# First stage of a fused attention and two-layer expert kernel: other places for weight conversions and input loads

## The chip, the cores and the metric

The kernel runs on one core of a Trainium2 chip. The metric is the device time of one execution in microseconds (us). Three runs of the kernel before the change gave 792.18, 792.83 (the median) and 796.73 us. The profile and every row below come from one profiled execution of 793.86 us, whose traced span is 792.0 us.

## The reference

Three layers follow each other; the output of one is the input of the next.

```
scores = q @ k.T / 8        # 4 batches, 8 heads, 576 tokens, 64 per head
                            # heads 0-3 see the last 32 tokens, heads 4-7 every fourth of the last 128
x = softmax(scores) @ v     # -> 2304 tokens x 512
x = (x @ w_a * (x @ w_b)) @ w_out          # 512 -> 1536 -> 512
e = argmax(normalised x @ expert_emb.T)    # 8 experts
out = gate * (relu(x @ w1[e]) @ w2[e])     # 512 -> 1024 -> 512
```

w_a, w_b and w_out arrive as 64-bit floating-point numbers, everything else as 32-bit ones. The kernel converts the 64-bit weights to 32 bits on the chip.

## The kernel before

**Batches and steps.** The work goes batch by batch. For batch b, `f_step(b, f, ...)` runs for the 12 blocks f of 128 hidden columns (n = 12 b + f numbers them through), and then `x1_run` multiplies by w_out. One `f_step` has four groups of 12 matmuls on TensorE, `mm(0,0)`, `mm(1,0)`, `mm(0,1)`, `mm(1,1)`: column half c of the weights (a or b) by token half hf, each product as three passes (high by high, high by low, low by high; lines 702 to 704). Each group fills one PSUM bank. `a_copy` (ACT, L739) empties the bank of the a half, `g_evac` (DVE, L745) multiplies it with the b half and so empties that bank; a later `g_lows` splits the product into a high part (ACT, L748) and a low part (POOL, L749).

**Attention inside the steps.** While batch b is in these steps, the attention of batch b + 1 is worked off in pairs of 64-query tiles (`AttnPair`; five pairs, the last one a single tile). In batch 0 a pair opens in an odd-numbered n (1, 3, 5, 7, 9: "even" in the code, since f - lag is even there) and goes on in the next. Its parts: `scores` (PE, into the banks sc and rps), `least_of` (maxima, DVE L536, then a small POOL operation, L544), `exp(i)` (four ACT exponentials per tile, L550), `norm(i)` (two small DVE operations, L557 and L558, then a POOL product, L559, over the tile s), `trans(i)` (four PE transposes into the single bank tp, L567, and an ACT copy out of it, L569), `av` (PE, L578), `oevac` (ACT L593, DVE L595). `trans(0)` stands in the second step of a pair, `trans(1)` at the head of the step after it. The attention of batch 0 itself runs ahead of the first step (class `Attn`, tiles j = 0 to 8, `trans` of tile i - 3 and `av` of tile i - 4 in turn i), with a few filler matmuls (`keep_warm`).

**Conversion of the weights, in batch 0 only.** `conv_load(i)` brings block i as 64-bit words (1024 KB). `conv_steps(i)` makes 32-bit numbers of it in four steps that `conv(cg, k)` takes k at a time: ACT scales the upper words in place (L640), DVE shifts (L642), DVE combines (L644), DVE combines again (L646). `conv_store` writes the result back to DRAM for the later batches. In step n, block n + 2 is converted; `ab_split(n+1)` splits the block converted in the step before into a high part (ACT, L660) and a low part (DVE, L661) in one of the two buffers "ab". The split of block 1 is done in step 0 in four parts, its low parts on POOL.

**What sets the order.** The order is written out by hand: every engine works its own instructions off strictly in the order of the code, and so does SP, which issues all loads and stores of this stage; a wait at the head of a queue holds all that is behind it. Semaphores between engines follow from the buffers. The PSUM banks and the bank tp exist once each. `load_qk` and `load_v` go through the input tiles (batch, third g): 832 KB and 576 KB each, two buffers each, so that a third one waits until an earlier tile has been used. `early_conv` converts blocks 0 and 1 during the attention of batch 0.

In the step that opens a pair ACT gets before the change: copy of `trans(1)`, L640, L660, L739, L593, L748, `exp(0)`, L748, L739; DVE gets L642, L661, maxima, L595, L644, L745, `norm(0)`, L745, L646.

Of the kernel before, what the change touches and what calls it, by code (L numbers as in the profile page):

```python
# [8 lines left out]
F32 = mybir.dt.float32  # L9
# [72 lines left out]
def fused_kernel(ctx: ExitStack, tc: tile.TileContext, qk, v, wab, wout, w1, w2, emb, tau, cst, msk, out, dbg=None):  # L82
# [279 lines left out]
    ap = ab_ctx.enter_context(tc.tile_pool(name="ab", bufs=2, side="right"))  # L362
    ld = attn_ctx.enter_context(tc.tile_pool(name="ld", bufs=2, side="right"))
# [9 lines left out]
    qkt, vt = {}, {}  # L373

    ld_seq = [(b, g) for b in range(B) for g in range(3)]
    ld_pos = [0, 0]

    def load_qk():
        if ld_pos[0] < len(ld_seq):
            b, g = ld_seq[ld_pos[0]]  # L380
            ld_pos[0] += 1
            qkt[b, g] = ld.tile([128, 4, 416], F32, tag="qk", name="qkt")
            nc.sync.dma_start(out=qkt[b, g], in_=qk[b, g])

    def load_v():
        if ld_pos[1] < len(ld_seq):
            b, g = ld_seq[ld_pos[1]]
            ld_pos[1] += 1
            vt[b, g] = ld.tile([96, 3, 512], F32, tag="v", name="vt")
            nc.sync.dma_start(out=vt[b, g], in_=v[b, g])  # L390

    x0 = {}
# [214 lines left out]
    def conv_load(i):  # L607
        if i < len(conv_src):
            if i < NF and i % 3 == 2:
                c64[i] = mp.tile([128, 2048], I32, tag="wo", name="c64w", bufs=1)  # L610
            elif i in (NF + 2, NF + 3):
                c64[i] = ap.tile([128, 2048], I32, tag="ab", name="c64a")
            else:
                c64[i] = cv.tile([128, 2048], I32, tag="c64", name="c64")
            nc.sync.dma_start(out=c64[i], in_=conv_src[i].bitcast(I32))
# [3 lines left out]
    def raw_tile(name):  # L619
        return mp.tile([128, 1024], F32, tag="raw", name=name, bufs=3)  # L620

    def conv_store():
        while conv_kept:
            keep, dst = conv_kept.pop(0)
            nc.sync.dma_start(out=keep, in_=dst)
# [24 lines left out]
    def conv(gen, n=4):  # L650
        for _ in range(n):
            next(gen, None)

    def ab_load(n):
        if NF <= n < n_ab:
            ab_raw[n] = raw_tile("abr")
            nc.sync.dma_start(out=ab_raw[n], in_=wab32[n % NF])
# [9 lines left out]
    def ab_split_part(n, q):  # L667
        if q == 0:
            ab_hl[n] = ab_tile()
        w = slice(256 * q, 256 * q + 256)  # L670
        split(ab_raw[n][:, w], ab_hl[n][0][:, w], ab_hl[n][1][:, w], eng=nc.gpsimd)
        if q == 3:
            ab_raw.pop(n)

    def ab_split(n):
        if n < n_ab:
            hl = ab_tile()
            split(ab_raw.pop(n), *hl)
            ab_hl[n] = hl
# [9 lines left out]
    def wo_split(n):  # L689
        if n < N_WO:  # L690
            if not wo_box:
                wo_box.append(mp.tile([128, 2, 2, 512], F32R, tag="wo", name="wo", bufs=1))
            hl = (wo_box[0][:, n % 2, 0, :], wo_box[0][:, n % 2, 1, :])
            w = slice(512 * (n % 2), 512 * (n % 2) + 512)
            split(wo_raw[n // 2][:, w], *hl, eng=nc.vector)
            if n % 2:
                wo_raw.pop(n // 2)
            wo_hl[n] = hl
# [9 lines left out]
    def ab_mm(n, acc, c, hf, k):  # L708
        hl = ab_hl[n]
        xh, xl = x0[n // NF]  # L710
        if k == 0:
            acc[c, hf] = ps.tile([128, HALF], F32, tag=f"mm{2 * hf + c}", name=f"mm{2 * hf + c}")
        w = slice((2 * k + c) * 128, (2 * k + c) * 128 + 128)
        t = slice(hf * HALF, hf * HALF + HALF)
        mm3(acc[c, hf], (hl[0][:, w], hl[1][:, w]), (xh[:, k, t], xl[:, k, t]), k == 0, k == 3)
# [7 lines left out]
    def f_step(b, f, pairs, extra, extra2):  # L723
        n = b * NF + f
        acc = acc_pre if n == 0 else {}
        lag = 1 if b == 0 else 0
        p, odd = divmod(f - lag, 2)
        cur = pairs[p] if 0 <= p < len(pairs) else None
        prv = pairs[p - 1] if not odd and 0 <= p - 1 < len(pairs) else None

        def mm(c, hf):
            for k in range(2 if (c, hf) in acc else 0, 4):
                ab_mm(n, acc, c, hf, k)

        kept = {}

        def a_copy(hf):
            kept[hf] = ap.tile([128, HALF], F32, tag="a", name="a")
            nc.scalar.activation(out=kept[hf], in_=acc[0, hf], func=AF.Copy)  # L739

        def g_evac(hf):
            g = ap.tile([128, HALF], F32, tag="g", name="g")
            c = hf * HALF + CARRY * (1 - b % 2)
            t = slice(c, c + HALF)
            nc.vector.tensor_tensor(out=g, in0=kept[hf], in1=acc[1, hf], op=ALU.mult)  # L745

            def low():
                nc.scalar.activation(out=g_hl[0][:, f, t], in_=g, func=AF.Copy)  # L748
                nc.gpsimd.tensor_tensor(out=g_hl[1][:, f, t], in0=g, in1=g_hl[0][:, f, t].bitcast(F32), op=ALU.subtract)  # L749

            g_low.append(low)

        if f - lag in (3, 6, 9):
            load_qk()
        if f - lag in (5, 8, 11):
            load_v()
        if f < NF - 2:
            ab_load(n + 2)
        if b == 0 and n < 10:
            conv_load(n + 4)  # L760
        if n == NF - 1:
            conv_load(NF + 2)
        if b == 0:
            conv_store()
        cg = iter(())
        if b == 0:
            cg = conv_steps(n + 2)
        if cur is not None and odd:
            conv(cg, 1)
            cur.exp(1)  # L770
            conv(cg, 1)
            cur.norm(1)
            conv(cg, 1)
        if prv is not None:
            prv.trans(1)
        if not odd or cur is None:
            conv(cg, 2)
        if n == 0:
            for q in range(4):
                ab_split_part(1, q)  # L780
        elif f < NF - 1:
            ab_split(n + 1)
        elif b == 0:
            wo_split(0)
        mm(0, 0)
        a_copy(0)
        if not odd:
            if cur is not None:
                cur.open()
            if prv is not None:  # L790
                prv.av()
            if cur is not None:
                cur.scores()
                cur.least_of()
            if prv is not None:
                prv.oevac()
            conv(cg, 1)
        g_lows()
        mm(1, 0)
        if cur is not None and not odd:  # L800
            cur.exp(0)
        g_evac(0)
        if cur is not None and odd:
            cur.trans(0)
        g_lows()
        for x in extra:
            x()
        mm(0, 1)
        a_copy(1)
        for x in extra2:  # L810
            x()
        mm(1, 1)
        if cur is not None and not odd:
            cur.norm(0)
        g_evac(1)
        del ab_hl[n]
        conv(cg)
# [347 lines left out]
    with tc.manual_schedule():  # L1165
# [17 lines left out]

        early_conv = conv_all()
        for i in range(NJ + LAG + 1):
            if i in (3, 6, 9):
                load_qk()
            if i in (4, 6, 9):
                load_v()
            if i == CONV1:  # L1190
                conv_load(1)
                nc.sync.dma_start(out=c_sb, in_=cst)
            if i == 6:
                conv_load(2)
            if i < NJ:
                gr[i].scores(early=True)
            if 1 <= i < NJ + 1:
                gr[i - 1].exp()
            if LAG <= i < NJ + LAG:
                gr[i - LAG].trans()  # L1200
                gr[i - LAG].tevac()
            if LAG + 1 <= i:
                gr[i - LAG - 1].av()
            keep_warm(N_WARM if i < 4 else N_WARM_LATE if i < WARM_TO else 0, "mm1" if (i + 1 - LAG) % 2 else "tp")
            if 1 <= i < NJ + 1:
                gr[i - 1].norm()
            if i == NJ + LAG:
                conv(early_conv, CONV_STEPS[i])
            if LAG + 1 <= i:
                gr[i - LAG - 1].oevac()  # L1210
            if i < NJ + LAG:
                conv(early_conv, CONV_STEPS[i])
            for q in range(4):
                if SPLIT0[q] == i:
                    ab_split_part(0, q)
            if i in PRE:
                for k in range(2):
                    ab_mm(0, acc_pre, PRE.index(i), 0, k)
        for _ in early_conv:
            pass  # L1220
        load_v()

        router = None
        for b in range(B):
# [10 lines left out]
            for f in range(NF):  # L1235
                extra = []
                extra2 = []
                if b == 1 and f == 0:
                    ebox.append(rbox_pool[0].tile([128, E1, DM], F32, tag="big", name="en_a"))
                    ebox.append(ap.tile([128, E - E1, DM], F32, tag="en_b", name="en_b", bufs=1))  # L1240
                    for t, e0 in zip(ebox, (0, E1)):
                        n = t.shape[1]
# [261 lines left out]
```

## Time and profile before

| | |
|---|---|
| runs | 792.18, 792.83, 796.73 us |
| profiled execution | 793.86 us, span 792.0 us |
| busy over the span | PE 774.6, PEld 723.5, DVE 518.8, ACT 410.1, POOL 206.2 us |
| opening, 0 to 62 us | PE busy 55.38 us, DVE 42.78, ACT 39.81, POOL 25.58; DMA 91% |
| rest of the first stage, 62 to 124 us | PE busy 62.00 us, DVE 52.48, ACT 42.96, POOL 27.20; DMA 77% |
| chain that ended last | PE 84% of the span, DMA 9%, issue 4%, DVE 1%, ACT 1% |

PE is TensorE's matmul side, PEld its weight loads, DVE VectorE, ACT ScalarE, POOL GpSimd, SP the queue that issues loads. Matmuls are pipelined and their ends are modelled, so a PE that is busy is not a PE at its peak. In rows of the timeline, the first number is the start in us from the span's start, the second the duration in us; a square bracket at the end gives the idle time of the engine just before and what ended it.

### The profile page before, as it was taken

The numbers are of one execution on the slowest core, as the hardware profiler recorded it, in microseconds if no ns is written. First come the engines' busy times: TensorE is split into PE (matmuls) and PEld (weight loads), VectorE is DVE, ScalarE is ACT, GpSimd is POOL, SyncE is SP. The second block draws the span as 40 slices with busy tenths as digits, with TensorE's granted clock in tenths as the row PEclk, the third lists the DMA queues.
The fourth block names the chain that finished last, engine by engine and source line by source line (L and its number), as shares of the span: only waits on it lengthen the run. The fifth ranks groups of instructions, "written<-read, shape, count | busy, mean of one in ns | idle before, by whom it ended". The sixth has DMA issues, their size and how long they took to land.

```text
span 792.0 us, 15979 instructions
## 1 busy us (share of the span) xinstructions
PE 774.6 (98%) x6122; PEld 723.5 (91%) x6122; DVE 518.8 (66%) x1155; ACT 410.1 (52%) x993; POOL 206.2 (26%) x251
## 2 busy tenths in 40 slices
PE   8989999999999999999999999999999999999995
PEld 4789998899999889999889999999898999999993
DVE  5788888758986228887627874455564566566570
ACT  5757774366653136665234443455463655665651
POOL 3454443023442204443222225331000001111110
PEclk9999999999999999999999999999999999999998
DMA  9987877497732323222152222635574554755720
GB/s 285 317 254 235 283 259 272 185 329 231 258 124 85 133 83 113 93 81 81 63 174 97 81 81 99 247 134 176 204 249 157 181 177 139 251 157 165 237 79 26
DMA packets 40294, 136.18 MB, mean 172 GB/s; under 512 B 4083, under 2 KB 4339, under 8 KB 37776
## 3 DMA queue, kind: packets, MB, share of 16 engines
q1 hardware_dynamic: 37120, 125.54, 48.4%
q0 software_dynamic: 3088, 9.52, 3.2%
q8 instruction: 50, 0.82, 0.4%
q14 instruction: 36, 0.29, 0.1%
HBM read 109.67 MB, written 25.80 MB: 171 GB/s over the span
## 4 chain that ended last, share of the span: by engine, by line
PE 84%; DMA 9%; issue 4%; DVE 1%; ACT 1%; POOL 0%; POOLq 0%; DVEq 0%; ACTq 0%
PE mm L702 13%; PE mm L703 12%; PE mm L704 12%; DMA out_dram<-yo,ixi 5%; PE xr L702 5%; PE xr L703 5%; PE xr L704 4%; PE hp L704 3%; PE hp L703 3%; PE hp L702 3%; PE av L578 2%; DMA c<-in_wab_dram 2%; PE ytp L703 2%; PE xm L704 2%; PE ytp L704 2%
## 5 line engine op out<-in xcount | busy, mean ns | idle before, releaser
L702 PE MATMUL mm<-x0h,ab 128*128 128x288 f32 x768 | 230.8, 301 | 1.0 <-DVE g L745 1.0
L704 PE MATMUL mm<-x0h,ab 128*128 128x288 f32 x768 | 226.5, 295 | 0.3 <-DVE ab L661 0.3
L703 PE MATMUL mm<-x0l,ab 128*128 128x288 f32 x768 | 226.2, 295 | 0.0
L702 PEld LDWEIGHTS mm<-x0h,ab 128*128 128x128 f32 x768 | 144.1, 188 | 3.5 <-DVE g L745 1.2
L704 PEld LDWEIGHTS mm<-x0h,ab 128*128 128x128 f32 x768 | 144.1, 188 | 0.9 <-DVE ab L661 0.5
L703 PEld LDWEIGHTS mm<-x0l,ab 128*128 128x128 f32 x768 | 144.2, 188 | 0.2
L749 POOL TENSOR_TENSOR gl<-g,gh 128x288 fp32r<-128x288 f32 x96 | 90.6, 946 | 131.6 <-ACT gh L748 128.6
L661 DVE TENSOR_TENSOR wl<-raw,wh 128x1024 fp32r<-128x1024 f32 x60 | 73.0, 1222 | 53.4 <-ACT wh L660 53.2
L661 DVE TENSOR_TENSOR wo<-wor,wo 128x512 fp32r<-128x512 f32 x60 | 47.0, 785 | 63.6 <-ACT wo L660 58.8
L660 ACT ACTIVATE wo<-wor 128x512 fp32r<-128x512 f32 x60 | 37.8, 631 | 86.0 <-PE xr L704 57.4
L1120 POOL DMA_INDIRECT out_dram<-yo,ixi x23 | 26.4, 1146 | 205.6 <-ACT yo L1119 160.3
L661 DVE TENSOR_TENSOR ab<-abr,ab 128x1024 fp32r<-128x1024 f32 x46 | 58.9, 1281 | 29.7 <-ACT ab L660 29.7
L745 DVE TENSOR_TENSOR g<-a,mm 128x288 f32<-128x288 f32 x96 | 43.2, 450 | 41.4 <-PE mm L704 17.0
L702 PE MATMUL hp<-xTh,wh 128*128 128x352 f32 (+6 forms) x224 | 68.9, 308 | 0.0
L748 ACT ACTIVATE gh<-g 128x288 fp32r<-128x288 f32 x96 | 42.9, 447 | 47.9 <-DVE g L745 47.4
L703 PE MATMUL hp<-xTl,wh 128*128 128x352 f32 (+6 forms) x224 | 67.7, 302 | 0.0
L704 PE MATMUL hp<-xTh,wl 128*128 128x352 f32 (+6 forms) x224 | 67.6, 302 | 0.0
L660 ACT ACTIVATE wh<-raw 128x1024 fp32r<-128x1024 f32 x64 | 67.1, 1054 | 0.0
L660 ACT ACTIVATE ab<-abr 128x1024 fp32r<-128x1024 f32 (+1 forms) x54 | 51.4, 961 | 23.2 <-PE mm L704 16.1
L702 PE MATMUL xr<-wo,gh 128*128 128x512 f32 x156 | 61.0, 391 | 0.0
L703 PE MATMUL xr<-wo,gh 128*128 128x512 f32 x156 | 60.9, 390 | 0.0
L704 PE MATMUL xr<-wo,gl 128*128 128x512 f32 x156 | 60.8, 390 | 0.0
(239 smaller groups left out, 1654.5 us busy)
## 6 DMA issues: line engine op xcount, KB each, us to landing
raw<-in_w_dram SPq DMA_DIRECT2D x64, 512.0 KB, 4.1
abr<-wab SPq DMA_DIRECT2D x36, 512.0 KB, 3.2
wor<-wout SPq DMA_DIRECT2D x24, 512.0 KB, 3.6
qkt<-in_qk_dram SPq DMA_DIRECT2D x12, 832.0 KB, 11.0
c<-in_wab_dram SPq DMA_DIRECT2D x8, 1024.0 KB, 11.4
vt<-in_v_dram SPq DMA_DIRECT2D x12, 576.0 KB
xs<-rows SPq DMA_DIRECT2D x8, 781.5 KB
wab<-abr SPq DMA_DIRECT2D x12, 512.0 KB, 6.4
```

What stands on the lines that cost most here:

```text
L578: nc.tensor.matmul(out=self.o[64 * p:64 * p + 64, pr, 64 * i:64 * i + 64], lhsT=t[:, jj, 64 * h:64 * h + 64], rhs=self.aT[i][:, pr, 64 * ( ...
L660: nc.scalar.activation(out=hi, in_=raw, func=AF.Copy)
L661: (eng or nc.vector).tensor_tensor(out=lo, in0=raw, in1=hi.bitcast(F32), op=ALU.subtract)
L702: nc.tensor.matmul(out=out_, lhsT=lh, rhs=rh, start=first, stop=False)
L703: nc.tensor.matmul(out=out_, lhsT=lh, rhs=rl, start=False, stop=False)
L704: nc.tensor.matmul(out=out_, lhsT=ll, rhs=rh, start=False, stop=last)
L745: nc.vector.tensor_tensor(out=g, in0=kept[hf], in1=acc[1, hf], op=ALU.mult)
L748: nc.scalar.activation(out=g_hl[0][:, f, t], in_=g, func=AF.Copy)
L749: nc.gpsimd.tensor_tensor(out=g_hl[1][:, f, t], in0=g, in1=g_hl[0][:, f, t].bitcast(F32), op=ALU.subtract)
L1120: nc.gpsimd.indirect_dma_start(out=out, out_offset=bass.IndirectOffsetOnAxis(ap=self.ixi[e][:m, t:t + 1], axis=0), in_=yo[:m, :], in_offse ...
```

## The change

It has three parts. The third v tile of batch 0 is put into a buffer of the kind "ab", so that it needs no free v buffer, and is loaded right behind the second. The loads of the second batch (its first v, and its second q/k tile) move behind the conversions of batch 0's attention, and its second v into step n = 2. In the steps of batch 0 the four conversion steps move: where a pair opens, L640 and L642 from ahead of `ab_split` to behind `exp(0)` and the first `g_evac`, and L644 from behind `oevac` to ahead of `norm(0)`; where a pair goes on, L640 from ahead of `exp(1)`, L642 from ahead of `norm(1)` and L644 from behind it, to behind `a_copy(0)` (L640 and L642) and the first `g_evac` (L644). L646 stays at the end of a step.

```diff
@@ load_v
-            vt[b, g] = ld.tile([96, 3, 512], F32, tag="v", name="vt")
+            if ld_pos[1] == 3:
+                vt[b, g] = ap.tile([128, 2048], F32, tag="ab", name="vt")[:96, :1536].rearrange("p (j c) -> p j c", j=3)
+            else:
+                vt[b, g] = ld.tile([96, 3, 512], F32, tag="v", name="vt")
@@ f_step
         if f < NF - 2:
             ab_load(n + 2)
+        if n == 2:
+            load_v()
...
         if cur is not None and odd:
-            conv(cg, 1)
             cur.exp(1)
-            conv(cg, 1)
             cur.norm(1)
-            conv(cg, 1)
         if prv is not None:
             prv.trans(1)
-        if not odd or cur is None:
+        if cur is None:
             conv(cg, 2)
...
             if prv is not None:
                 prv.oevac()
-            conv(cg, 1)
+            if cur is None:
+                conv(cg, 1)
+        elif cur is not None:
+            conv(cg, 2)
         g_lows()
         mm(1, 0)
         if cur is not None and not odd:
             cur.exp(0)
         g_evac(0)
+        if cur is not None:
+            conv(cg, 1 if odd else 2)
         if cur is not None and odd:
             cur.trans(0)
         g_lows()
...
         mm(1, 1)
         if cur is not None and not odd:
+            conv(cg, 1)
             cur.norm(0)
         g_evac(1)
         del ab_hl[n]
         conv(cg)
@@ attention of batch 0
-            if i in (3, 6, 9):
+            if i == 3:
                 load_qk()
-            if i in (4, 6, 9):
+            if i == 4:
+                load_v()
                 load_v()
             if i == CONV1:
                 conv_load(1)
+            if i == 6:
+                load_qk()
+                conv_load(2)
                 nc.sync.dma_start(out=c_sb, in_=cst)
-            if i == 6:
-                conv_load(2)
...
         for _ in early_conv:
             pass
+        load_qk()
         load_v()
```

## Rows read from the trace of the kernel before

**Rows 1.** Windows: stretch, length, busy us per engine, granted clock, DMA share, GB/s.
```profile
20.00:40.00 20.00, 18.48 (x219) 14.32 (x217) 14.55 (x39) 14.75 (x58) 9.29 (x15) 1.00 1.03 315
...
50.00:55.00 5.00, 3.44 (x25) 3.20 (x26) 4.78 (x9) 4.75 (x16) 3.91 (x4) 1.00 0.46 119
60.00:80.00 20.00, 20.00 (x249) 19.38 (x244) 17.44 (x32) 14.69 (x45) 9.04 (x11) 1.00 0.77 244
```

**Rows 2.** Timeline of PE: start, duration, line; idle before in brackets.
```profile
28.70 0.28 PE L474 MATMUL av<-aT,vt 96*64 96x64 f32 x2 [1.03 <-DMA vt<-in_v_dram]
...
53.41 0.31 PE L567 MATMUL atp<-ident,s 128*96 128x128 f32 x1 [1.29 <-POOL s L559]
...
57.10 0.27 PE L567 MATMUL atp<-ident,s 128*96 128x128 f32 x1
...
69.50 0.27 PE L567 MATMUL atp<-ident,s 128*96 128x128 f32 x1
...
73.14 0.27 PE L567 MATMUL atp<-ident,s 128*96 128x128 f32 x1
```

**Rows 3.** Chain of waits in the opening: start, duration, what.
```profile
19.73 8.83 DMA vt<-in_v_dram
...
29.68 14.62 DMA c<-in_wab_dram
```

**Rows 4.** Timeline of ACT: the first conversion inside the steps, its wait in brackets.
```profile
44.32 1.13 ACT L640 ACTIVATE c<-c 128x1024 f32<-128x1024 f32 x1 [4.17 <-DMA c<-in_wab_dram]
```

**Rows 5.** Timeline of DVE: last steps of two conversions in the opening.
```profile
27.72 1.51 DVE L646 SCALAR_TENSOR_TENSOR abr<-c,abr 128x1024 uint32<-128x1024 uint32 x1
...
42.45 1.23 DVE L646 SCALAR_TENSOR_TENSOR abr<-c64w,abr 128x1024 uint32<-128x1024 uint32 x1
```

**Rows 6.** Timeline of DVE in steps 5 to 7.
```profile
85.37 0.16 DVE L557 TENSOR_SCALAR asm<-asm 128x4 f32<-128x4 f32 x1
...
90.22 1.22 DVE L646 SCALAR_TENSOR_TENSOR abr<-c64w,abr 128x1024 uint32<-128x1024 uint32 x1
91.52 0.69 DVE L642 TENSOR_SCALAR abr<-c 128x1024 uint32<-128x1024 uint32 x1
92.57 1.22 DVE L661 TENSOR_TENSOR ab<-abr,ab 128x1024 fp32r<-128x1024 f32 x1 [0.35 <-ACT ab L660]
93.71 0.35 DVE L536 TENSOR_REDUCE amx<-sc 128x2 f32<-128x192 f32 x1
```

**Rows 7.** Timeline of ACT in steps 5 to 7.
```profile
82.00 0.39 ACT L739 ACTIVATE a<-mm 128x288 f32<-128x288 f32 x1
82.29 1.15 ACT L640 ACTIVATE c64w<-c64w 128x1024 f32<-128x1024 f32 x1
...
86.20 0.44 ACT L748 ACTIVATE gh<-g 128x288 fp32r<-128x288 f32 x1
86.53 0.58 ACT L569 ACTIVATE aT<-atp 96x512 f32<-96x512 f32 x1
...
91.47 1.06 ACT L660 ACTIVATE ab<-abr 128x1024 fp32r<-128x1024 f32 x1
92.44 0.39 ACT L739 ACTIVATE a<-mm 128x288 f32<-128x288 f32 x1
...
94.74 0.34 ACT L550 ACTIVATE s<-sc,least 128x96 f32<-128x96 f32 x1 [0.73 <-POOL least L544]
```

**Rows 8.** Timeline of POOL: its products in step 5, and one in step 6.
```profile
79.35 0.82 POOL L749 TENSOR_TENSOR gl<-g,gh 128x288 fp32r<-128x288 f32 x1
...
82.94 0.82 POOL L559 TENSOR_TENSOR s<-s,asm 128x384 f32<-128x384 f32 x1
...
85.91 1.63 POOL L559 TENSOR_TENSOR s<-s,asm 128x384 f32<-128x384 f32 x1 [2.15 <-PE atp L567]
```

**Rows 9.** Timeline of DVE at the same times.
```profile
79.84 1.42 DVE L644 SCALAR_TENSOR_TENSOR abr<-c,abr 128x1024 uint32<-128x1024 uint32 x1
...
83.05 1.80 DVE L646 SCALAR_TENSOR_TENSOR abr<-c,abr 128x1024 uint32<-128x1024 uint32 x1
```

## The prediction

> **What bounds the kernel now.** I read the windows first, then PE's timeline, then the chain of waits, and last ACT, DVE and POOL side by side. The windows split the stage in two. From 60 to 80 us PE is busy without a gap, while DVE is busy for 17.4 of 20 us; from 50 to 55 us PE works only 3.4 of 5 us [rows 1]. In the steps a pair of attention tiles repeats: the first transpose after a pair stands at 57.10 and at 73.14, so a pair of steps takes **16.04 us**, and PE sets that; within it the other transpose follows after 12.40 us (69.50) [rows 2]. So only the opening has time to give: PE waits 1.03 us at 28.70 for the third v tile, and 1.29 us at 53.41 for the normalised scores [rows 2]. The chain of waits names two loads behind these: the v tile, 8.83 us from issue to landing, and conversion block 3, 14.62 us [rows 3]. Block 3 holds ACT idle for 4.17 us until 44.32 [rows 4], with the split of block 2 and the copy that frees a bank queued behind it.
>
> **The opening.** The third v tile is now issued near 11 us instead of 19.73. It overtakes block 1 and a q/k tile (1024 and 832 KB); at the 315 GB/s of this stretch [rows 1] that is 6 us, so it lands near 22 and PE goes on at 27.6, where the work before it ends: 1.1 us gained there. Not all of it passes on. Block 0's conversion ends at 29.23 (27.72 + 1.51 [rows 5]) with or without the tile, and the first weights' split stands behind it. I take **0.9 us** at step 1, with 0.5 and 1.1 as ends. The overtaken block 1 comes 576 KB, so 1.9 us, later; that hides while it lands ahead of 30 us, and by the order of the queue it lands near 26. Block 3 no longer has 1.4 MB of second-batch tiles ahead of it, lands some 5 us earlier, near 39, and its wait goes: first use is now near 47. The second batch's tiles that moved back are first used from step 3 on, near 60; their cover is over 10 us. Putting v into a weights buffer delays the split of block 1 only if the last attention product came after it; it comes 4 us before. The v load in step 2 stands on SP ahead of block 6's load, which waits longer anyhow. I cost these at nothing.
>
> **The steps: what each moved conversion lands on.** The cost sits in the queues. Today ACT does L640 in gaps in which it would wait anyway for the previous L646. Afterwards L640 stands behind exp(0), and L642, which needs it, stands on DVE ahead of L644, norm(0), the second g_evac and L646; the next split waits for that L646. I follow this loop from one end of L646 to the next, each link from two neighbouring starts.
>
> Step that opens a pair: L646 ends, L660 after 0.03 (90.22 + 1.22 to 91.47), L661 after 1.10, maxima after 1.14, exp(0) after 1.03 [rows 6, 7]. Four exponentials of 0.34 that overlap a little: 1.3. L640 and the hand-over to L642: 1.18; L642: 0.69 [rows 6, 7].
>
> Here the trace shows that DVE and POOL exclude each other. L646 lasts 1.22 us alone [rows 6] and 1.80 us when it starts 0.11 us after POOL's product; it ends 1.09 us after that product does. L644 beside the other product: 1.42 us, again 1.09 us after its end [rows 8, 9]. In the new order L748 runs behind L640, so POOL's low part (L749) comes up while L642 is running, gets in at its end, and holds L644: 0.82 + 1.09. Then norm(0) to POOL's product 0.54 (85.37 to 85.91), the product 0.82, and L646, held by it, 1.09 more [rows 6, 8]. Sum: 0.03 + 1.10 + 1.14 + 1.03 + 1.3 + 1.18 + 0.69 + 0.82 + 1.09 + 0.54 + 0.82 + 1.09 = 10.83; less some 0.15 for instructions of one engine that overlap by about 0.08 (L661 ends 0.08 after the maxima begin [rows 6]): **10.7 us**.
>
> Step that goes on: L660 0.03, L739 0.97, L640 0.29, L642 1.18, its run 0.69, POOL's low part 0.82, L644 1.09, the second low part 0.82, L646 1.09 [rows 6 to 9]: 6.98, about **6.9 us**.
>
> The loop is 17.6 us where PE needs 16.04. So DVE, ACT and POOL together become the bound of the stage: **+1.56 us per pair**. On PE it shows in two places: trans(0) waits for the product s, and trans(1) for the copy out of the bank tp, now behind L640 on ACT.
>
> The Trainium skill, page "SBUF — State Buffer", section "Who interferes with whom", has this as a rule: VectorE with two SBUF inputs and a GpSimd operation that reads SBUF lock each other out for the whole instruction, in order of issue. The trace agrees (1.80 against 1.22 us). It speaks against this change: by it the loop is the one above, without it the one of rival 1.
>
> **The sum.** Step 1: -0.9. Block 2's L646 then ends at 42.75 (42.45 + 1.23 - 0.9 [rows 5]); trans(0) of the first pair comes 9.6 us later, near 52.4, where it is at 53.41 [rows 2]: -1.0. L646 ends near 53.5; on ACT follow L660 and L739 (0.03 + 0.97 + 0.29), L640 (1.05), L748 (0.33) and the copy (0.58) [rows 7], so trans(1) stands near 56.8 instead of 57.10: **-0.3**. Three more intervals of 1.56 to step 9: +4.4. The last pair has one tile, so PE reaches its transpose sooner, and waits about 1.2 us: **+5.6**; I take +5.4 for the hand-overs rounded up. From step 11 on PE is the bound again and no later stage has slack to give it back. 793.86 + 5.4 = 799.3 for the profiled execution; the median of the runs shown is 1.03 us below that one, hence **798.2 us**.
>
> The ends of this case: the opening gains 0.5 or 1.1, the loop is 17.3 to 17.9: 796.6 to 800.4.
>
> **The rivals.**
> 1. PE stays the bound. If low parts and products slip past DVE without collisions, the loop is 9.35 + 6.2 = 15.5 us: L644 1.12 and L646 1.22 in place of the held ones, no waits for POOL. Then 16.04 holds, trans(0) of the first pair comes at 51.6 instead of 53.41, and -1.8 stays to the end: **791.0**, faster than now by 0.2%. Decisive: whether the loop is under 16.04. For it: POOL is busy for 9 of 20 us only [rows 1]. Against it: in the present order one of these collisions or another is in every row pair I read [rows 8, 9].
> 2. The order of norm(0)'s product and L646 turns. They come up within 0.1 us of each other. With L646 first the product waits, but the loop is 17.0: +0.95 per pair, later transposes by 1.2 us once. -0.3 + 2.9 + 1.2 = +3.8, so **796.6**.
> 3. PE's clock. All windows read show a granted clock of 1.00, the 2.4 GHz level, also where PE stands still for 1.3 us between bursts [rows 1, 2]. The new wait at the first trans(0) is one piece of about 3 us in place of several short ones: the matmuls ahead of it, which nothing delays any more, are done near 49.3, and it comes at 52.4. Were the clock to fall to 1.2 GHz there, the 24 matmuls behind it (3.6 us from 53.41 to 57.10 [rows 2]) would take up to twice as long: +3.6 on top, **801.8**, and more if later waits do it too. Nothing in the rows shows such a fall. The Trainium skill, "TensorE: Matmul & The Clock Gate", section "HAM oscillation — how this bites in real kernels", says that waits between bursts can bring the half clock; no row before the end of the kernel shows it.
> 4. The change does not reach what it is for: v lands no earlier since the queue of loads is full (DMA share 1.03 [rows 1]). Then 0.9 is lost and the loop stays: 799.1, inside the forecast's range.
>
> **The chances.** About 1% (7.9 us) is what a measurement of this kernel can tell from no change. The forecast has 0.52 with its variant 4, rival 1 has 0.22, rival 2 0.17, rival 3 0.06; 0.03 is left for what I don't see. Range: from rival 1's 790.6 (0.4 more gained in the opening) to 800.4, which leaves out rival 3 and some of the edges. Slower by over 1% means above 800.8: rival 3 and the upper tail, 0.11. Faster by over 1% would need 784.9; PE's waits in the opening add up to less than 7 us (3.44 of 5 us and 18.48 of 20 us busy in the worst windows [rows 1]), so 0.02. Within 1%: 0.87.
>
> **What would show it.** In the changed profile: the v wait at the third tile's first product is gone, and L640 of block 3 starts without waiting for a load. Then, in each pair, PE idle ahead of L567 on POOL's s, and at the head of the next pair on the copy L569; L644 and L646 at 1.4 to 1.9 us; transposes at the head of a pair 17 to 18 us apart instead of 16.04. Gaps of 16.04 with no idle PE after 60 us mean rival 1; 17.0 means rival 2; a granted clock under 1 between 50 and 60 us rival 3. The prediction is wrong in its core if DVE is idle in these steps while L640 waits for nothing.

## The result, and the profile after

The changed kernel takes **799.69 us** in the median of eight runs (799.07 to 804.38); the kernel before takes 792.44 us in eight (791.35 to 796.73). The ratio is **1.0101, 95% interval 1.0084 to 1.0118**: slower by 6.7 to 9.4 us. The interval takes in 1%, the bound that the prediction drew between "within" and "slower". Ratios here come from runs side by side, so they are not exactly the quotient of the medians. The kernel before varies more than the differences that some experiments are after: in 80 later runs of it, the 25 whose mean granted clock was under 0.995 took 795.1 us in the median, the 55 others 791.9.

| | before | after |
|---|---|---|
| profiled execution | 793.86 us, span 792.0 | 799.91 us, span 798.1 |
| busy PE / DVE / ACT / POOL | 774.6 / 518.8 / 410.1 / 206.2 us | 776.4 / 520.9 / 409.1 / 200.4 us |

The busy time of PE, DVE and ACT is the same to about 2 us, and POOL's is 5.8 us less; what was added is waiting. Lines of the changed kernel are 3 higher: L643 is the L640 of before, L645, L647 and L649 are L642, L644 and L646, L663 and L664 the split, L751 and L752 the parts of g, L562, L570 and L572 the product s, the transpose and the copy.

The same windows as in [rows 1], of the changed kernel (stretch, length, busy us of PE, PEld, DVE, ACT, POOL, granted clock, DMA share, GB/s):

```profile
20.00:40.00 20.00, 19.52 (x227) 15.10 (x223) 14.85 (x40) 14.88 (x58) 9.86 (x16) 1.00 0.89 307
50.00:55.00 5.00, 2.40 (x11) 2.36 (x12) 4.04 (x8) 2.08 (x9) 1.93 (x3) 0.72 0.52 107
60.00:80.00 20.00, 19.30 (x247) 18.38 (x245) 15.24 (x24) 13.30 (x38) 6.31 (x8) 1.00 0.65 211
```

From 20 to 40 us PE is busy for 1.04 us more; from 60 to 80 us it is no longer full, and neither is any other engine. So no engine's busy time alone is the bound there any more; that a chain through several engines is, the rows below and the experiments have to show. PE's timeline at the transposes, beside [rows 2] (start, duration, and in brackets the idle time before and what ended it):

```profile
52.60 1.09 PE L570 MATMUL atp<-ident,s 128*96 128x128 f32 x4 [2.86 <-POOL s L562]
57.65 0.60 PE L570 MATMUL atp<-ident,s 128*96 128x128 f32 x4
70.06 0.60 PE L570 MATMUL atp<-ident,s 128*96 128x128 f32 x4
74.55 0.61 PE L570 MATMUL atp<-ident,s 128*96 128x128 f32 x4 [0.70 <-ACT aT L572]
87.32 0.64 PE L570 MATMUL atp<-ident,s 128*96 128x128 f32 x4 [0.19 <-POOL s L562]
91.79 0.61 PE L570 MATMUL atp<-ident,s 128*96 128x128 f32 x4 [0.63 <-ACT aT L572]
104.56 0.64 PE L570 MATMUL atp<-ident,s 128*96 128x128 f32 x4 [0.19 <-POOL s L562]
109.04 0.61 PE L570 MATMUL atp<-ident,s 128*96 128x128 f32 x4 [0.64 <-ACT aT L572]
121.80 0.64 PE L570 MATMUL atp<-ident,s 128*96 128x128 f32 x4 [0.68 <-POOL s L562]
```

The transposes behind a pair, at the head of the next step (`trans(1)`, here called the heads), stand at 74.55, 91.79 and 109.04: **17.24 and 17.25 us** apart, where PE needed 16.04. PE waits in the two places that were forecast, for s and for the copy out of tp. DVE over one pair, beside [rows 6, 9]:

```profile
76.36 1.46 DVE L649 SCALAR_TENSOR_TENSOR abr<-c,abr 128x1024 uint32<-128x1024 uint32 x1
...
83.56 0.69 DVE L645 TENSOR_SCALAR abr<-c 128x1024 uint32<-128x1024 uint32 x1 [1.05 <-ACT c L643]
84.29 1.71 DVE L647 SCALAR_TENSOR_TENSOR abr<-c,abr 128x1024 uint32<-128x1024 uint32 x1
...
86.60 1.75 DVE L649 SCALAR_TENSOR_TENSOR abr<-c,abr 128x1024 uint32<-128x1024 uint32 x1
...
90.88 0.69 DVE L645 TENSOR_SCALAR abr<-c64w 128x1024 uint32<-128x1024 uint32 x1
...
91.85 1.46 DVE L647 SCALAR_TENSOR_TENSOR abr<-c64w,abr 128x1024 uint32<-128x1024 uint32 x1
...
93.60 1.46 DVE L649 SCALAR_TENSOR_TENSOR abr<-c64w,abr 128x1024 uint32<-128x1024 uint32 x1
```

POOL over the same pair, beside [rows 8]:

```profile
83.93 0.99 POOL L752 TENSOR_TENSOR gl<-g,gh 128x288 fp32r<-128x288 f32 x1 [1.55 <-ACT gh L751]
86.44 0.83 POOL L562 TENSOR_TENSOR s<-s,asm 128x384 f32<-128x384 f32 x1 [1.52 <-DVE asm L561]
...
91.25 0.98 POOL L752 TENSOR_TENSOR gl<-g,gh 128x288 fp32r<-128x288 f32 x1 [1.61 <-ACT gh L751]
92.49 1.49 POOL L752 TENSOR_TENSOR gl<-g,gh 128x288 fp32r<-128x288 f32 x1 [0.26 <-ACT gh L751]
```

Every one of the four big combining steps of a pair runs beside a POOL operation and takes 1.46 to 1.75 us instead of 1.22 [rows 6]; each ends 1.08 us after POOL's operation does (83.93 + 0.99 = 84.92, and 84.29 + 1.71 = 86.00). And DVE stands idle for 1.05 us because L643 now runs behind exp(0). ACT, beside [rows 4, 7]:

```profile
47.74 1.15 ACT L643 ACTIVATE c<-c 128x1024 f32<-128x1024 f32 x1
...
82.39 1.13 ACT L643 ACTIVATE c<-c 128x1024 f32<-128x1024 f32 x1
83.42 0.44 ACT L751 ACTIVATE gh<-g 128x288 fp32r<-128x288 f32 x1
...
95.09 1.06 ACT L663 ACTIVATE ab<-abr 128x1024 fp32r<-128x1024 f32 x1 [1.90 <-DVE abr L649]
```

Block 3's conversion (47.74) waits for no load now, and neither does the third v tile's first product: PE's wait of 1.03 us there is gone. L751 at 83.42 waits behind L643, so POOL's low part comes up while DVE is in L645: as forecast. The split at 95.09 waits 1.90 us for L649 and closes the loop.

Where the 6.1 us of the two spans lie, at four places on PE: the first transpose comes at 52.60 against 53.41 (-0.81), the one of step 10 at 121.80 against 117.15 (+4.65), the first product with w_out at 132.66 against 127.97 (+4.69), the transposes that follow that stage at 164.34 against 158.37 (**+5.97**), and from there on it stays within 0.2 us of that. So 5.46 us come from the four intervals of the loop, and 1.3 us are lost in the w_out product of batch 0, which the forecast didn't have. The ends of that product, first after, then before:

```profile
164.34 0.41 PE L158 MATMUL etp<-ident,esb 8*128 8x8 f32 x4
```

```profile
158.37 0.41 PE L158 MATMUL etp<-ident,esb 8*128 8x8 f32 x4
```

The one wait of PE that the timeline marks in this product:

```profile
136.68 0.50 PE L706 MATMUL xr<-wo,gh 128*128 128x512 f32 x1 [0.41 <-DVE wo L664]
```

What it waits for, on DVE after:

```profile
134.80 1.22 DVE L649 SCALAR_TENSOR_TENSOR wor<-c,wor 128x1024 uint32<-128x1024 uint32 x1
135.94 0.69 DVE L664 TENSOR_TENSOR wo<-wor,wo 128x512 fp32r<-128x512 f32 x1
```

and the same two on DVE before:

```profile
128.64 1.22 DVE L646 SCALAR_TENSOR_TENSOR wor<-c,wor 128x1024 uint32<-128x1024 uint32 x1
129.78 1.30 DVE L661 TENSOR_TENSOR wo<-wor,wo 128x512 fp32r<-128x512 f32 x1
```

The conversion is 6.16 us late where PE is 4.69 us late: DVE came out of the steps with a backlog of 1.5 us over PE's. The marked wait is 0.41 us of the 1.3; the rest lies mainly in three matmuls that start 0.80 us (this one), 0.53 us (at 139.84) and 0.49 us (at 133.61) after the one ahead, where 0.23 is usual. Before, only two starts there are late, by 0.3 us together.

### The profile page after: what moved, and what is told of

It reads as the page before. It is cut to its first block, busy times and chain, and to the rows that moved or that the text cites. A ratio compares the mean times of both kernels' runs of the same rounds, so it can differ in the third digit from the quotient of the medians.

```text
span 798.1 us, 15980 instructions
## 1 busy us (share of the span) xinstructions
PE 776.4 (97%) x6122; PEld 724.2 (91%) x6122; DVE 520.9 (65%) x1155; ACT 409.1 (51%) x993; POOL 200.4 (25%) x251
## 4 chain that ended last, share of the span: by engine, by line
PE 72%; DMA 5%; issue 3%; DVE 1%; ACT 0%; POOLq 0%; POOL 0%; DVEq 0%
PE mm L705 10%; PE mm L706 10%; PE mm L707 10%; DMA out_dram<-yo,ixi 5%; PE xr L706 4%; PE xr L705 4%; PE xr L707 4%; PE hp L707 3%; PE hp L706 3%; PE hp L705 3%; PE xm L707 2%; PE ytp L706 2%; PE ytp L707 2%; PE ytp L705 2%; PE xm L705 2%
## 5 line engine op out<-in xcount | busy, mean ns | idle before, releaser
L752 POOL TENSOR_TENSOR gl<-g,gh 128x288 fp32r<-128x288 f32 x96 | 90.6, 947 | 139.0 <-ACT gh L751 139.0
L664 DVE TENSOR_TENSOR wl<-raw,wh 128x1024 fp32r<-128x1024 f32 x60 | 73.0, 1222 | 53.3 <-ACT wh L663 53.1
L664 DVE TENSOR_TENSOR wo<-wor,wo 128x512 fp32r<-128x512 f32 x60 | 46.5, 776 | 63.6 <-ACT wo L663 61.6
L664 DVE TENSOR_TENSOR ab<-abr,ab 128x1024 fp32r<-128x1024 f32 x46 | 56.5, 1227 | 38.7 <-ACT ab L663 38.5
L663 ACT ACTIVATE wo<-wor 128x512 fp32r<-128x512 f32 x60 | 37.8, 630 | 85.1 <-PE xr L707 59.7
L663 ACT ACTIVATE ab<-abr 128x1024 fp32r<-128x1024 f32 (+1 forms) x54 | 51.3, 959 | 48.6 <-DVE abr L649 17.9
L663 ACT ACTIVATE wh<-raw 128x1024 fp32r<-128x1024 f32 x64 | 67.0, 1054 | 0.0
L751 ACT ACTIVATE gh<-g 128x288 fp32r<-128x288 f32 x96 | 42.8, 446 | 35.5 <-DVE g L748 35.0
```

The costliest lines, as they stand in the source:

```text
L663: nc.scalar.activation(out=hi, in_=raw, func=AF.Copy)
L664: (eng or nc.vector).tensor_tensor(out=lo, in0=raw, in1=hi.bitcast(F32), op=ALU.subtract)
```

## The experiments

The theory: in the new order ACT, DVE and POOL form a loop longer than PE's work, its length made by POOL's reads holding DVE (**loop, with the port in it**). Rivals: the moved loads do it (**loads**); PE's clock, which fell here (0.72 from 50 to 55 us), does it (**clock**). Open besides: which half of the pair, which moved step, and what the 1.3 us behind step 11 are (**backlog**). The texts of what was expected call the first one the queue theory, and its part on POOL's reads the port theory.

**e1_loads**: the loads alone.

```diff
@@ against the kernel before
-            vt[b, g] = ld.tile([96, 3, 512], F32, tag="v", name="vt")
+            if ld_pos[1] == 3:
+                vt[b, g] = ap.tile([128, 2048], F32, tag="ab", name="vt")[:96, :1536].rearrange("p (j c) -> p j c", j=3)
+            else:
+                vt[b, g] = ld.tile([96, 3, 512], F32, tag="v", name="vt")
...
+        if n == 2:
+            load_v()
...
-            if i in (4, 6, 9):
+            if i == 4:
+                load_v()
                 load_v()
...
```

> Only the load part of the change, conversions where they were before. Queue theory (the moved conversions make a loop through ACT, DVE and POOL of 17.2 us per pair): no loop, pairs stay 16.04 us apart; the third v tile and conversion block 3 come early, so the waits before the transposes of step 2 (28.70, 50.28 and 53.41 us before) go or shrink: 3 us faster than before (2 to 3.6), and no fall of the granted clock. Load theory (the second batch's loads, moved later, cost the time): slower than before by 3 us or more, with PE waiting for q/k or v tiles in steps 3 to 9. Clock theory (the fall to 0.83 between 50 and 60 us is the cost): no long wait, no fall, 1 to 3 us faster.

Measured: 791.48 us against 792.37, ratio 0.997 (0.9949 to 0.9992). PE, in the profile of e1_loads:

```profile
50.42 0.64 PE L570 MATMUL atp<-ident,s 128*96 128x128 f32 x4 [1.29 <-POOL s L562]
54.10 0.60 PE L570 MATMUL atp<-ident,s 128*96 128x128 f32 x4
66.50 0.60 PE L570 MATMUL atp<-ident,s 128*96 128x128 f32 x4
70.14 0.60 PE L570 MATMUL atp<-ident,s 128*96 128x128 f32 x4
```

Pairs are 16.04 us apart (54.10, 70.14) and the span is 789.0. The loads are no cause of the loss. The gain is small and loosely known: 3 us were expected, the interval says 0.6 to 4.0 us, the medians 0.9; the spans differ by 3.0, but the profiled execution of before is a long one. No version that was run is clearly faster than this one.

**e2_conv**: the conversions alone, the loads as before.

```diff
@@ against the kernel after
-        if n == 2:
-            load_v()
...
-            if i == 4:
-                load_v()
+            if i in (4, 6, 9):
                 load_v()
...
```

> Only the moved conversions, loads as before. Queue theory: the loop is there, transposes 17.2 us apart from step 5 on, and the opening loses what the early v tile gave (0.6 us): 0 to 1 us slower than the changed kernel, 7 to 9 us slower than before. Load theory: about as before, at most 1 us slower. Clock theory: slower than before if PE again waits in one piece of over 2 us ahead of step 2's transposes and the clock falls; about as before if the clock stays at 1.00.

Measured: 801.92 us against 792.37, ratio 1.0113 (1.0079 to 1.0148); its profiled execution was the lowest of its six runs, 799.67. The median is 2.2 us above that of the changed kernel, where 0 to 1 us was expected; the lowest run is level with it. PE, in the profile of e2_conv:

```profile
52.66 0.64 PE L567 MATMUL atp<-ident,s 128*96 128x128 f32 x4 [2.92 <-POOL s L559]
57.14 0.61 PE L567 MATMUL atp<-ident,s 128*96 128x128 f32 x4 [0.64 <-ACT aT L569]
69.92 0.64 PE L567 MATMUL atp<-ident,s 128*96 128x128 f32 x4 [0.20 <-POOL s L559]
74.39 0.61 PE L567 MATMUL atp<-ident,s 128*96 128x128 f32 x4 [0.64 <-ACT aT L569]
```

and its window around the long wait:

```profile
50.00:60.00 10.00, 6.70 (x60) 6.26 (x62) 8.92 (x13) 5.24 (x14) 4.38 (x5) 1.00 0.52 168
```

The loop is there in full (17.25 us) without the loads. And the wait is as long as in the changed kernel while the granted clock stays at 1.00, the 2.4 GHz level: already here the clock is not needed for the loss.

**e3_open** and **e4_goon**: the conversions moved in one half of the pairs only.

```diff
@@ e3_open against the kernel after
         if cur is not None and odd:
+            conv(cg, 1)
             cur.exp(1)
+            conv(cg, 1)
             cur.norm(1)
+            conv(cg, 1)
...
-        elif cur is not None:
-            conv(cg, 2)
...
-        if cur is not None:
-            conv(cg, 1 if odd else 2)
+        if cur is not None and not odd:
+            conv(cg, 2)
@@ e4_goon against the kernel after
-        if cur is None:
+        if not odd or cur is None:
             conv(cg, 2)
...
-            if cur is None:
-                conv(cg, 1)
+            conv(cg, 1)
...
-        if cur is not None:
-            conv(cg, 1 if odd else 2)
+        if cur is not None and odd:
+            conv(cg, 1)
...
-            conv(cg, 1)
             cur.norm(0)
```

> The changed kernel with the conversions moved only in the steps that open a pair; in the steps that go on they stand as before. Queue theory: the opening step's part of the loop (10.5 us from one L646 end to the next) holds the excess, the other step needs about 6.6 us in either order: loop near 17.1, 5 to 7 us slower than before. If both steps shared the blame it would be half, 2 to 4 us slower. Load theory: as the changed kernel, 7 to 8 us slower.

> The changed kernel with the conversions moved only in the steps that go on with a pair; in the steps that open one they stand as before. Queue theory: the loop is 9.3 + 6.7, about 16, so PE stays the bound: as fast as with the loads alone, 2 to 3.5 us faster than before. If both steps shared the blame: 2 to 4 us slower than before. Load theory: as the changed kernel, 7 to 8 us slower.

Measured: e3 797.97 us, ratio 1.0064 (1.0045 to 1.0084), transposes at the heads at 56.14, 73.20, 90.33: 17.1 us apart. e4 791.46 us, ratio 0.9977 (0.9958 to 0.9996), heads 16.04 apart (54.16, 70.20), one wait of 1.29 us for s in all. PE, in the profile of e3_open:

```profile
73.20 0.64 PE L570 MATMUL atp<-ident,s 128*96 128x128 f32 x4
90.33 0.64 PE L570 MATMUL atp<-ident,s 128*96 128x128 f32 x4
```

The change in the opening step alone makes the loop longer than PE's work; the one in the going-on step alone costs nothing that can be seen, and adds about 0.14 us per pair on top of the other.

**e5_act_back**: ACT's L643 back ahead of the split in the opening steps, all the rest as after.

```diff
         if cur is None:
             conv(cg, 2)
+        elif not odd:
+            conv(cg, 1)
...
-            conv(cg, 1 if odd else 2)
+            conv(cg, 1)
```

> The changed kernel, but in the steps that open a pair ACT's conversion step alone goes back ahead of the split (into the time in which ACT waits for the last conversion); the three DVE steps stay where the change put them. Queue theory: the link from exp(0) over ACT's conversion to DVE's shift goes, 1.1 us of the 10.5, and the low part of g comes a little sooner; the loop falls to 15.8 to 16.1 and PE is the bound again: 2 to 3.5 us faster than before, transposes 16.04 apart. If instead the place of the DVE steps or the port alone makes the loop: 4 to 8 us slower than before.

Measured: 793.37 us against 792.39, ratio 1.0 (0.9983 to 1.0017). The heads of pairs are 16.37, 16.19 and 16.20 us apart. This one step is worth 1.05 us per pair of the 1.2, and 6.3 us between the medians of the two kernels. The total still missed what was expected (2 to 3.5 us faster than before): the loop stays a little over 16.04, and the opening still has waits of 1.42 and 0.65 us on PE. POOL's hold on DVE is still there too; how much of the rest it makes was not tested apart. DVE in the profile of e5_act_back:

```profile
79.77 0.69 DVE L645 TENSOR_SCALAR abr<-c 128x1024 uint32<-128x1024 uint32 x1
80.50 1.80 DVE L647 SCALAR_TENSOR_TENSOR abr<-c,abr 128x1024 uint32<-128x1024 uint32 x1
```

and POOL:

```profile
80.42 0.81 POOL L752 TENSOR_TENSOR gl<-g,gh 128x288 fp32r<-128x288 f32 x1 [0.68 <-ACT gh L751]
```

POOL starts 0.08 us ahead of L647, which takes 1.80 us; the wait of L645 for L643 (1.05 us after) is gone.

**e6_no_read**: in batch 0 POOL writes zeros where it computed the low part of g, and reads nothing (that low part is left out of the result).

```diff
+                if b == 0:
+                    nc.gpsimd.memset(g_hl[1][:, f, t].bitcast(F32), 0.0)
+                else:
                     nc.gpsimd.tensor_tensor(out=g_hl[1][:, f, t], in0=g, ...)
```

> The changed kernel, but in batch 0 POOL writes zeros into the low part of g in place of reading g and its high part (left out: the low part of batch 0's products). POOL then reads nothing from SBUF there. Port theory (VectorE with two SBUF inputs and a POOL operation that reads SBUF lock each other out): L647 falls from 1.7 to 1.2 us where a pair opens and from 1.46 to 1.2 where it goes on, L649 from 1.46 to 1.2 where it goes on, and stays at 1.7 beside the product s; loop 17.24 down to about 16.3; 3.5 to 5.5 us faster than the changed kernel, 2 to 4 slower than before. If the longer durations have another cause, or POOL's writes lock as well: as the changed kernel, 7 to 8 us slower than before.

Measured: 794.11 us against 792.39, ratio 1.0011 (0.9995 to 1.0027): 5.6 us below the changed kernel and 1.7 above the one before, both just outside what was expected (3.5 to 5.5 and 2 to 4). Pairs are 16.57, 16.31 and 16.33 apart. DVE in the profile of e6_no_read:

```profile
81.09 1.23 DVE L647 SCALAR_TENSOR_TENSOR abr<-c,abr 128x1024 uint32<-128x1024 uint32 x1
...
82.88 1.81 DVE L649 SCALAR_TENSOR_TENSOR abr<-c,abr 128x1024 uint32<-128x1024 uint32 x1
...
85.88 1.23 DVE L664 TENSOR_TENSOR ab<-abr,ab 128x1024 fp32r<-128x1024 f32 x1 [0.90 <-ACT ab L663]
...
88.21 1.22 DVE L647 SCALAR_TENSOR_TENSOR abr<-c64w,abr 128x1024 uint32<-128x1024 uint32 x1
...
89.71 1.22 DVE L649 SCALAR_TENSOR_TENSOR abr<-c64w,abr 128x1024 uint32<-128x1024 uint32 x1
```

and POOL:

```profile
82.78 0.83 POOL L562 TENSOR_TENSOR s<-s,asm 128x384 f32<-128x384 f32 x1 [3.83 <-DVE asm L561]
...
85.92 0.62 POOL L753 MEMSET gl<- 128x288 f32 x2
```

Where POOL no longer reads, three of the four steps fall to 1.22; the one beside the product s, which still reads, stays at 1.81. So both L643's new place and POOL's reads are needed for the long loop: either one undone takes it to 16.2 or 16.3.

**e8_filler**: fourteen filler matmuls on PE ahead of the waiting transpose in step 2, so that PE doesn't stand still there.

```diff
+        if n == 2:
+            keep_warm(14, "tp")
             cur.trans(0)
```

> The changed kernel with 14 filler matmuls (3.0 us) on PE in step 2, ahead of the transpose that waits 2.9 us, so that PE works through the wait. Queue theory: the granted clock stays at 1.00 between 50 and 60 us, and the time is that of the changed kernel within 0.7 us, since the loop of DVE, ACT and POOL sets when steps 3 to 10 end. Clock theory: 1.5 to 3.5 us faster than the changed kernel.

Measured: 799.78 us against 792.39, ratio 1.0093 (1.006 to 1.0127), heads 17.25 us apart (74.11, 91.36). Its window:

```profile
50.00:60.00 10.00, 9.51 (x89) 7.66 (x89) 8.81 (x13) 4.86 (x12) 4.13 (x4) 1.00 0.61 182
```

The clock stays at 1.00 and the time is that of the changed kernel: the clock falls as a cause.

**e10_half**: the conversions moved up to step 6 only, the loads as after.

```diff
@@ against the kernel after
+        old = n >= 7
...
+            conv(cg, old)
             cur.exp(1)
+            conv(cg, old)
             cur.norm(1)
+            conv(cg, old)
...
-        if cur is None:
+        if cur is None or (old and not odd):
             conv(cg, 2)
...
-        if cur is not None:
+        if cur is not None and not old:
             conv(cg, 1 if odd else 2)
...
```

> The changed kernel, with the conversions moved only up to step 6; from step 7 on they stand as before. Queue theory, with a backlog: up to step 7 the transposes at the head of a pair are 17.2 us apart, then 16.04; the 1.3 us that the changed kernel loses once more in the product with w_out of batch 0 were left-over conversions, so they go too: 2 to 3.3 us slower than before. If these 1.3 us have a cause of their own, the other loads or the buffer parity: 3.5 to 4.5 us slower than before. If the loop has momentum of its own and goes on in the old order: 6 us or more.

Measured: 796.04 us against 792.54, ratio 1.0042 (1.0022 to 1.0062). The time does not decide: 3.3 us by the ratio and 3.5 by the medians are the near ends of the two forecasts (2 to 3.3 and 3.5 to 4.5). The traces do. How late step 10's transpose and the transposes behind the w_out product are, against the profile of before (117.15 and 158.37):

| | step 10 | behind w_out | paid in between |
|---|---|---|---|
| after | +4.65 | +5.97 | +1.32 |
| e2_conv | +4.50 | +5.80 | +1.30 |
| e3_open | +3.68 | +4.13 | +0.45 |
| e10_half | +2.33 | +2.13 | -0.20 |
| e4_goon | -2.94 | -2.94 | 0.00 |

With the old order from step 7 on, nothing is paid behind step 10, where all three kernels that run the long loop to its end pay. That is what the backlog says; the wait for wo above is where it is paid. That e2 pays as much as the changed kernel clears the moved loads. e4 has the moved order in step 10 too, but no long loop, and pays nothing. But e3, with a loop of 17.1 us and the old order in the going-on steps, pays only 0.45: the full 1.3 us was seen only where the loop is long and both kinds of steps are moved. Why e3 pays less was not tested.

**e7_best** and **e9_norm_first**: two tries to get more out of e1. Both keep e1's order but put step 1's L647 behind norm(0); e9 also puts norm(0) ahead of POOL's low part of that step's first g.

```diff
@@ e7_best against e1_loads
-            conv(cg, 1)
+            conv(cg, 0 if n == 1 else 1)
@@ e9_norm_first against e7_best
         g_evac(0)
+        if n == 1:
+            cur.norm(0)
...
-        if cur is not None and not odd:
+        if cur is not None and not odd and n != 1:
             cur.norm(0)
```

> The loads alone, with one more edit: in step 1 DVE's third conversion step stands behind the normalisation, so that POOL's product for the first transpose of step 2 does not come up behind it and the second low part. With the loads alone PE waits 1.29 us for that product at 50.42. Queue theory: the wait goes or falls under 0.4 us, 0.9 to 1.4 us faster than the loads alone, 3 to 4 us faster than before. If the product is then held by another step: as the loads alone.

> The kernel e7_best, with the normalisation of step 1 queued on POOL ahead of the low part of the step's first g. There the product s came up 0.09 us behind DVE's L647 and was held by it, so that PE waited 1.18 us at 49.97. Queue theory: s now runs from about 47.5 to 48.3, ahead of L647, the wait goes and the pair's first transpose stands near 48.8: 0.9 to 1.3 us faster than e7_best and than the loads alone, near 3.5 us faster than before. If the port is not what held it: as e7_best.

Measured: e7 792.24 against 792.39, ratio 0.9982 (0.9966 to 0.9999); e9 792.02 against 792.54, ratio 0.9992 (0.998 to 1.0004). Both missed: neither beats e1. In e7 L647 started at 48.02 and the product s came up at 48.11, so this time POOL was held (1.81 us), and PE's wait for s stayed at 1.18 us. In e9 the first transpose came without a wait, but PE then waited 1.45 us at the next. PE in the profile of e9_norm_first:

```profile
49.01 0.60 PE L570 MATMUL atp<-ident,s 128*96 128x128 f32 x4
54.26 0.64 PE L570 MATMUL atp<-ident,s 128*96 128x128 f32 x4 [1.45 <-POOL s L562]
```

The wait was handed on, not removed.

## Why the prediction was right and wrong

- **The loop: right.** The part of the step that opens a pair, from the end of L649 at 77.82 to the next at 88.35, is 10.53 us (forecast 10.7), that of the step that goes on, to 95.06, is 6.71 (6.9); together 17.24 against 17.6. The difference is mainly one term: POOL's low part was put at 0.82 us behind the step that it follows. It comes up while that step still runs, and ends 0.67 us behind it (84.92 against 84.25, the end of L645; 93.98 against 93.31, the end of L647). Three such terms make 0.45 us, against a difference of 0.36. Four intervals cost 5.46 us where the sum had 6.4. One sign of being wrong was badly put: "if DVE is idle in these steps while L640 waits for nothing". DVE is idle for 1.05 us ahead of L645 while L643 waits for nothing, and the forecast's own sum has that idle time, as L642 there comes behind exp(0) and L640. The port rule of the Trainium skill ("SBUF — State Buffer", "Who interferes with whom") was rightly weighed in: without it the sum was rival 1, which fell; e6 agrees also in that an operation of POOL that only writes holds nothing (L664 at 85.88 takes 1.23 us beside the MEMSET).
- **The opening: nearly.** From the end of block 2's conversion (41.86 + 1.23) to the first transpose it is 9.51 us, where 9.6 was carried over; step 1 gained 0.59 us (L649 at 41.86 against 42.45) and not 0.9. But that wait for the v tile was partly chance: in e2, whose loads are those of before, it is 0.30 us and not 1.03, and block 2's step stands at 41.87 as well. Eight experiments have the moved loads and nothing changed before step 1; there the same step starts between 40.92 and 41.75. The forecast priced a wait for a load from one execution as if it were fixed.
- **The failed step** is "From step 11 on PE is the bound again and no later stage has slack to give it back". It asked only whether the loss could shrink, and put the growth at nothing without a reason. The loss grew by 1.3 us, as the conversion of a w_out block was 6.16 us late where PE was 4.69. Here the loop left DVE's queue behind PE's, and that was paid where PE first needed what DVE owed. By luck this term and the loop's 0.9 us too much have opposite signs: +6.05 between the profiled executions, +5.4 forecast. The second term that was mis-sized is the step from the profiled execution to the median: 1.03 us was taken off, and after the change it is 0.22. Of the 1.5 us between 798.2 and 799.69, 0.8 come from this one, and 0.6 are what the traces have over the forecast (6.05 against 5.4).
- **Within 1% or above: far too sure, though the range held the time.** The forecast had 0.87 on "within 1%" and 0.11 above. Its sum was 2.6 us short of that bound (798.2 against 800.8). Two things that come to this size together had no price: the backlog, and the base. The profiled execution of before lies 1.42 us above the median of its eight runs, that of after 0.22 above; the forecast took 1.03 off both. So +6.05 in the traces is +7.25 between the medians. By the interval (6.7 to 9.4 us) the result is on the bound and on neither side of it, but clearly slower; a good part of the 0.87 belonged above. The ends of the forecast's case, 796.6 and 800.4, are up to 0.6 us wider than its terms give (0.3 us of loop in four intervals, and 0.2 or 0.4 us of opening).
- **The rivals.** 1 (PE stays the bound) falls with 17.24. 2 (L646 ahead of the product) falls: the product starts at 86.44, L649 at 86.60. 3: the clock did fall where it was said, and at first it cost about 0.5 us (the head at 57.65, in e2 at 57.14); but e2 waits 0.64 us at that head, and the next one stands at 74.55 against 74.39. The 0.5 us is gone one pair later, since the loop sets when that transpose comes, so the +3.6 was wrong even with the clock down. 4 falls: PE no longer waits for the tile.

## What to carry to other kernels

An engine that is busy for two thirds of the time is no reserve if its work sits in a chain through three queues that work strictly in order: walk the chain from one end of a step to the next, count every hand-over, and compare that length with the bound engine's period. What such a loop delays can be more than what the engine that was the bound shows; ask where the other engines' arrears are paid. And when a forecast lies within 2 or 3 us of a bound, price the base too: the profiled execution of before lay 1.42 us off its median here, and one of its waits for a load, 1.03 us, was 0.30 us in another execution.

## What the runs showed of the hardware

- A wait of 2.86 us on PE was followed in the changed kernel by a granted clock of 0.72 from 50 to 55 us, a mean between the levels of 1.2 and 2.4 GHz, and the 128x288 matmuls behind it started 0.24 us apart instead of 0.13. In e2, e3 and e10 waits of 2.92, 2.87 and 2.86 us at the same place left it at 1.00; what made the difference is open. The Trainium skill, "TensorE: Matmul & The Clock Gate", section "HAM oscillation — how this bites in real kernels", says that PE waits between bursts can bring the half clock; the trace of the changed kernel agrees, the three others don't show it.
- Which of DVE and POOL goes first was settled by 0.08 to 0.16 us here (the starts 80.42 against 80.50 in e5, 48.02 against 48.11 in e7, 86.44 against 86.60 after), and the loser ran 0.5 to 1.0 us longer (1.80 for 1.22; 1.81 for 0.83).
